# Two batches by four heads: regrouping the units of an fp32 RWKV-5 recurrence ahead of a hierarchical mixture of experts, with its start-up, gate loads and last expert reordered

## The chip, the cores and the metric

The kernel runs on one core of one Trainium2 chip. The metric is device time in microseconds (us) for one launch. The profile comes from one separate execution of the same program. All arithmetic is fp32.

## What is computed

The first block is the RWKV-5 recurrence with B=4 batches, H=8 heads, S=768 tokens and D=48 channels per head. For each batch and head:

```python
for t in range(S):
    cur = outer(u * k[t], v[t])            # the token's own term
    y[t] = r[t] @ (state + cur)
    state = w[:, None] * state + outer(k[t], v[t])
```

The result, read as x of 3072 tokens by 384 channels (8 heads of 48), goes into a mixture of 16 experts, in 4 groups of 4. A token takes the group with the largest of `x @ w_group`, then in that group the expert with the largest of `x @ w_expert[g]`. Both softmax weights multiply the result of its one expert, `relu(x @ w1) @ w2`, with 1024 hidden channels. Tokens have to be sorted by expert, and the results scattered back into their places.

## The kernel before

The recurrence is cut into chunks of 128 tokens. 24 units, or steps `s = 0..23`, stand in a loop `for s in range(NT)`. A unit is one batch, eight heads, 128 tokens; two units make a group `g = s // 2`, and the groups alternate between batches 0, 1 and batches 2, 3. The order of instructions on every engine is the order of the program text, written out by hand. Work of several units is interleaved: step s ends the products of unit s while it prepares units s+1 to s+4.

A unit goes through these functions:

- `load` (L323) issues two DMAs for each of r, k and v, one for each batch, with rows of 48 floats (192 bytes).
- On GpSimd (POOL), `own` (L489, L490) forms r*k*u and `scaled` (L493) forms k times the table `T2` of inverse powers of w.
- On TensorE (PE), `turn` (L511) transposes k and r; ScalarE (ACT) copies kT out (L520) and VectorE (DVE) multiplies rT by the powers `pw` (L522).
- `scores` (L536) forms k'r for each head, written as four quadrant products: two head halves `e` (48 of 64 rows each) by two key halves `z`. The lower key half (z=0) has 128 query columns, the upper (z=1) only 64, since key 64 and later don't reach an earlier query.
- `diagonal` (ACT, L561) and `diagonal_here` (DVE, L553) put the own term on the diagonal of `am`; `mask` (DVE, L543) copies the scores into `am` where the key is earlier than the query.
- `state` (L574) multiplies rT with the carried state R and `values` (L583) adds am times v; `values_out` (ACT, L612) copies the sum to `yT`. `update` (L594) and `carry` (DVE, L604) renew R.
- `rows_out` (L630, ACT L634) turns yT into rows of x. `gate_parts` (L619) multiplies yT by the gates' weights `gwp` in four matmuls and copies the result `lT` (L624). In a later step `gate_sum` (L644) sums its quarters into logits. `route_1` to `route_5` then choose the expert, and POOL scatters the rows into `x_sorted` with an indirect DMA (L230).

The constant `CLOSE` is 5: up to that step one unit less lies in preparation. PE has PSUM areas named PA, YB, MS, TR, RW, SB and LG; turns of k use TR and turns of r RW. PE, DVE and ACT each have one order and no dynamic choice.

Four DMAs, issued by `fill` (L439) at s = 5, 6, 7 and 8, zero parts of `x_sorted`, 392 KB each. `gates_in` (L406, L409) loads the gates' weights with five DMAs whose rows are 16 bytes. A check whether w is in the range that the kernel can treat is `out_of_range` (L752, L753) at s=0, summed over partitions by a matmul, `all_out_of_range` (L756). `turn_nothing` (L422) issues transposes whose results are not used.

At the end of the recurrence the experts run, 16 in an order fixed at run time by the counts. Their products are L1104 (up) and L1116 (down), their results leave by indirect DMAs (L1128). The last expert has few rows: `rows_down` (L240) multiplies, ACT scales (L244), and one indirect DMA of POOL (L245) writes rows of 384 floats to `out`.

## Time and profile before

| | us |
|---|---|
| median of 3 runs | 400.97 |
| lowest, highest | 399.18, 401.94 |
| the profiled execution, its own time | 402.09 |
| span of the profiled execution | 400.3 |
| TensorE busy (share of the span) | 388.7 (97%) |
| POOL busy | 201.0 (50%) |
| ACT busy | 180.4 (45%) |
| DVE busy | 153.4 (38%) |
| first and last `values` of the recurrence start at | 12.14, 127.36 |
| first expert product starts at | 129.48 |

PE is the matmul engine and PEld its loading of weights, which the profile lists apart. SP is the engine that issues most DMAs, and SPq the time that its queue took for them. A line of the timeline gives start and duration, engine, line of the code, operation, `out<-in`, tile shapes and, in brackets, how long the engine stood idle ahead of it and what ended that. Durations are those of one execution.

### The profile page before, as it was taken

How to read it: one execution, taken by the hardware profiler on the slowest of the kernel's cores; microseconds unless marked ns; L12 is line 12 of the kernel's file. 1: busy time of each engine (PE TensorE's matmuls, PEld its weight loads, DVE VectorE, ACT ScalarE, POOL GpSimd, SP SyncE). 2: the span in 40 equal slices, each digit the busy share in tenths (PEclk: the TensorE clock that was granted, in tenths of full speed). 3: DMA queues.
4: the chain of work that ended last, by engine and by line, in shares of the span. 5: the costliest groups of instructions: out<-in, count | busy, mean ns of one | idle time of the engine just before them, and what ended most of it. 6: DMA issues, size and time to landing. Idle time of an engine off the chain costs nothing.

```text
span 400.3 us, 10467 instructions
## 1 busy us (share of the span) xinstructions
PE 388.7 (97%) x3963; PEld 361.9 (90%) x3963; DVE 153.4 (38%) x405; ACT 180.4 (45%) x429; POOL 201.0 (50%) x265
## 2 busy tenths in 40 slices
PE   8999999999999999999999999999999999999992
PEld 6787899999888977899999999999999999999981
DVE  7887988888867602101202112111121221211110
ACT  4665888888875211432433424424244244244210
POOL 7999956999842412105162351532624524523542
PEclk9999999999999999999999999999999999999999
DMA  8998999995965977999999999999989999981000
GB/s 159 160 174 159 197 208 221 212 195 147 264 200 123 308 193 212 233 275 258 232 258 243 228 250 266 224 253 284 200 240 259 255 247 268 233 236 28 27 18 27
DMA packets 123118, 81.80 MB, mean 204 GB/s; under 512 B 96863, under 2 KB 114289, under 8 KB 123061
## 3 DMA queue, kind: packets, MB, share of 16 engines
q1 hardware_dynamic: 116019, 71.12, 77.1%
q0 software_dynamic: 4752, 9.55, 8.1%
q8 instruction: 32, 0.52, 0.6%
q10 hardware_dynamic: 2290, 0.40, 0.5%
q14 instruction: 25, 0.20, 0.2%
HBM read 69.89 MB, written 11.67 MB: 204 GB/s over the span
## 4 chain that ended last, share of the span: by engine, by line
issue 46%; PE 29%; POOL 18%; SPq 3%; DVE 2%; DMA 1%; POOLq 1%; ACT 0%
POOL out_dram L1128 16%; PE YB L583 6%; PE PA L536 6%; SPq L323 3%; PE TR L511 3%; PE YB L574 2%; PE YB L630 2%; PE RW L511 2%; PE MS L594 2%; PE TR L619 2%; PE MS L644 1%; DMA vt<-in_v_dram 1%; POOL out_dram L245 1%; PE TR L793 1%; DVE am L543 1%
## 5 line engine op out<-in xcount | busy, mean ns | idle before, releaser
L1128 POOL DMA_INDIRECT out_dram<-yt,idn x93 | 90.4, 972 | 137.1 <-DVE yt L1126 107.0
L1076 DVE STREAM_TRANSPOSE xe<-xg 128x672 f32<-128x672 f32 (+2 forms) x16 | 12.7, 796 | 121.0 <-DMA xg<-x_sorted 88.7
L1116 PE MATMUL YB<-hT,w2p 128*128 128x208 f32 (+10 forms) x336 | 58.7, 328 | 0.0
L1116 PE MATMUL PA<-hT,w2p 128*128 128x208 f32 (+10 forms) x336 | 58.1, 326 | 0.0
L1116 PEld LDWEIGHTS YB<-hT,w2p 128*128 128x128 f32 x336 | 55.8, 190 | 0.0
L1116 PEld LDWEIGHTS PA<-hT,w2p 128*128 128x128 f32 x336 | 55.3, 190 | 0.0
L561 ACT ACTIVATE am<-ident,du 128x128 f32<-128x128 f32 x152 | 50.5, 398 | 0.0
L1125 DVE STREAM_TRANSPOSE yt<-yT 128x672 f32<-128x672 f32 (+1 forms) x14 | 11.8, 842 | 80.4 <-ACT yT L1119 80.4
L1094 ACT COPY w2p<-w 128x1024 f32<-128x1024 f32 x42 | 41.1, 1045 | 3.0 <-DMA w<-in_moe_w_dram 3.0
L543 DVE COPY_PREDICATED am<-later,PA 128x1024 f32<-128x1024 int32 x24 | 31.7, 1323 | 10.8 <-PE PA L536 6.1
L1104 PE MATMUL MS<-xe,w 128*128 128x208 f32 (+12 forms) x192 | 32.8, 320 | 0.0
L1104 PE MATMUL TR<-xe,w 128*128 128x208 f32 (+12 forms) x192 | 32.8, 320 | 0.0
L1104 PE MATMUL RW<-xe,w 128*128 128x208 f32 (+12 forms) x192 | 32.8, 320 | 0.0
L1104 PE MATMUL SB<-xe,w 128*128 128x208 f32 (+12 forms) x192 | 32.7, 320 | 0.0
L1104 PEld LDWEIGHTS SB<-xe,w 128*128 128x128 f32 x192 | 30.8, 190 | 0.6 <-issue 0.2
L1104 PEld LDWEIGHTS MS<-xe,w 128*128 128x128 f32 x192 | 30.7, 190 | 0.0
L1104 PEld LDWEIGHTS RW<-xe,w 128*128 128x128 f32 x192 | 30.7, 190 | 0.0
L1104 PEld LDWEIGHTS TR<-xe,w 128*128 128x128 f32 x192 | 30.7, 190 | 0.0
L230 POOL DMA_INDIRECT x_sorted<-xt,place_i x16 | 16.1, 1003 | 23.6 <-DVE end L719 11.8
L536 PE MATMUL PA<-rT,kT 48*64 48x128 f32 (+1 forms) x736 | 25.6, 255 | 0.5 <-issue 0.5
L583 PE MATMUL YB<-am,vt 128*48 128x128 f32 x384 | 25.9, 277 | 0.1
L490 POOL TENSOR_TENSOR dg<-dg,ub 128x384 f32<-128x384 f32 x24 | 24.1, 1003 | 1.9
(220 smaller groups left out, 560.1 us busy)
## 6 DMA issues: line engine op xcount, KB each, us to landing
w<-in_moe_w_dram SPq DMA_DIRECT2D x128, 384.0 KB, 9.5
vt<-in_v_dram SPq DMA_DIRECT2D x24, 192.0 KB, 4.5
rp<-in_r_dram SPq DMA_DIRECT2D x23, 192.0 KB, 4.3
kt<-in_k_dram SPq DMA_DIRECT2D x22, 192.0 KB, 5.2
xg<-x_sorted SPq DMA_DIRECT2D x36, 85.8 KB, 10.3
x_sorted<-zeros SPq DMA_DIRECT2D x4, 392.0 KB, 4.7
out_dram<-yt,idn POOLq DMA_INDIRECT x93, 7.5
xg<-x_sorted SPq DMA_DIRECT2D x20, 73.5 KB, 8.9
```

The costliest lines, as they stand in the source:

```text
L230: ins = nc.gpsimd.indirect_dma_start(out=xs_dram, out_offset=bass.IndirectOffsetOnAxis(ap=place_i[:, i : i + 1], axis=0), in_=xt[:, i].rea ...
L490: nc.gpsimd.tensor_mul(dg, dg, ub)
L511: nc.tensor.transpose(ps[:, hc, :], two, ident)
L536: nc.tensor.matmul(PA[64 * z : 64 * (z + 1), e, P * hc + 64 * z : P * (hc + 1)], lhsT=kT[rows, hc, 64 * z : 64 * (z + 1)], rhs=rT[rows, hc ...
L543: nc.vector.copy_predicated(am[n % NAM], later.unsqueeze(1).unsqueeze(1).to_broadcast([P, 2, HC, P]).bitcast(I32), PA.rearrange("p e (h t) ...
L561: nc.scalar.mul(am[n % NAM][:, e, hc, :], ident, dus[n][:, i : i + 1])
L583: nc.tensor.matmul(y_at(e, hc), lhsT=vt[:, n % 2, 2 * hc + e, :], rhs=amn[:, e, hc, :], start=(n < 4 and hc < 2), stop=True, skip_group_ch ...
L1076: nc.vector.transpose(xe[:, :, 0:nb, :], xg[:, 0:nb, 0:QW].rearrange("p i (ko a) -> p ko i a", a=32))
L1094: nc.scalar.copy(o4[:, kk], v4[:, kk])
L1104: nc.tensor.matmul(ph[:, i, 0:n], lhsT=w1[:, ko, P * (f + i) : P * (f + i + 1)], rhs=xe[:, ko].rearrange("p i b -> p (i b)")[:, 0:n], star ...
L1116: nc.tensor.matmul(po[:, 0:n], lhsT=w2p[:, d, fo, :], rhs=hT[:, fo, 0:n], start=(fo == 0), stop=(fo == FO - 1))
L1128: ins = nc.gpsimd.indirect_dma_start(out=out_q, out_offset=bass.IndirectOffsetOnAxis(ap=idn[:, i : i + 1].bitcast(U32), axis=0), in_=yt[:, ...
```

## The change

The change regroups the units. A unit is now two batches by four heads (`hf = n % 2` says which four), and a group still has two units. In the second batch the two 64-token halves of a chunk lie swapped on the partitions. So for two of a unit's four pairs of heads (`hc` 0, 1: first batch) the lower 64 partitions hold the earlier tokens, and for the other two (`hc` 2, 3) the later ones. What follows from that in the code:

- `load_heads` issues three DMAs for a tensor of a group: 128 rows of the first batch, and twice 64 rows of the second. For group 0, r and k are split by heads as well.
- `scores` computes, by `columns_of`, 64 or 128 columns in each quadrant, in the order of heads 0, 2, 1, 3; the mask `LT` has four tables, the powers `PW`, `IW` and `T2` two. ACT makes the swapped ones by copies.
- `gate_parts` treats two units at once, in odd steps, and `gate_sums` two chunk columns, in even steps. In steps 3 and 4 both stand behind `state`; at s=5 the sums follow `gate_parts`' place. At s=22 `part` is issued alone.
- `own`, `scaled`, `sum_own`, `head` and `rows_out` take the new indices; `own` takes a buffer for each unit rather than for each group (three of them as before). `tok4`, the token numbers, is made by four iotas instead of one.

Beside it:

- `gates_in` loads the gates' weights as long rows (768 bytes) with two DMAs, earlier in SP's order; `gates_turned` turns them with four PE transposes and two ACT copies.
- The `turn_nothing` calls between the turns are gone (the first 13 transposes stay, into PA); `rows_of_table` makes the second half of T2 after `scores(0)`.
- ACT's copies that fill pads and blank `am` buffers move, in part to s=1.
- At s=4 `values_out` follows the diagonals, and the turn of k for unit 7 goes to PA.
- The zero fill of s=8 is issued at s=7, with the third.
- `out_of_range` moves to s=8 and its sum joins the count at s=14 (`count_and_range`); `in_range` and `go_on` follow there and at s=17.
- For the last expert `half_down` computes 192 columns at a time, each half scaled and scattered by itself.

The diff, cut to its core:

```diff
...
+    def half_down(hT, w2, i, n, z, po, yt):
+        cols = slice(DM // 2 * z, DM // 2 * (z + 1))
+        for fo in range(FO):
+            nc.tensor.matmul(
+                po[0:n, 0 : DM // 2], lhsT=hT[:, fo, 0:n], rhs=w2[:, fo, cols], start=(fo == 0), stop=(fo == FO - 1),
+                skip_group_check=True,
+            )
+        nc.scalar.mul(yt[0:n], po[0:n, 0 : DM // 2], tagA[i][0:n, 1:2])
...
-        def load_half(t, src, g, a, queue):
-            c, b = g // 2, 2 * (g % 2) + a
-            queue.dma_start(out=t[:, a], in_=src[b, :, P * c : P * (c + 1), :].rearrange("h t d -> t h d"))
+        def load_heads(t, src, g, queue, heads=slice(0, H)):
+            for b in range(2):
+                for rows, t0 in ((slice(0, P), 0),) if b == 0 else ((slice(0, 64), 64), (slice(64, P), 0)):
+                    t1 = P * (g // 2) + t0
+                    queue.dma_start(
+                        out=t[rows, b, heads],
+                        in_=src[2 * (g % 2) + b, heads, t1 : t1 + rows.stop - rows.start, :].rearrange("h t d -> t h d"),
+                    )
 
         def load(src, g, name, bufs):
             t = place(g, name, bufs)
-            for a in range(2):
-                load_half(t, src, g, a, nc.sync)
+            load_heads(t, src, g, nc.sync)
...
+        gates = kp[3].rearrange("p a h x -> p (a h x)")[0 : H * G + H, 0 : D * Eg].rearrange("p (d x) -> p d x", x=Eg)
+
+        def gates_in():
+            nc.sync.dma_start(
+                out=gates[0 : H * G].rearrange("p d x -> p (d x)"),
+                in_=moe_w_expert.rearrange("g (h d) x -> (g h) (d x)", d=D),
+            )
+            nc.sync.dma_start(
+                out=gates[H * G :].rearrange("p d x -> p (d x)"), in_=moe_w_group.rearrange("(h d) x -> h (d x)", d=D)
...
-        def gates_in():
-            wg = moe_w_group.rearrange("(h d) g -> d h g", d=D)
-            nc.sync.dma_start(out=gwp[0:D, :, 0:G], in_=wg)
-            for g in range(G):
-                we = moe_w_expert[g].rearrange("(h d) x -> d h x", d=D)
-                nc.sync.dma_start(out=gwp[0:D, :, G + Eg * g : G + Eg * (g + 1)], in_=we)
+        def gates_turned():
+            n = H * G + H
+            ps = MS.rearrange("p (x c) -> p x c", c=P)
+            for x in range(Eg):
+                nc.tensor.transpose(ps[0:D, x, 0:n], gates[:, :, x], ident[0:n, 0:n])
+            nc.scalar.copy(
+                gwp[0:D, :, G : G + GE].rearrange("p h (g x) -> p x g h", x=Eg),
+                ps[0:D, :, 0 : H * G].rearrange("p x (g h) -> p x g h", h=H),
+            )
+            nc.scalar.copy(gwp[0:D, :, 0:G].rearrange("p h x -> p x h"), ps[0:D, :, H * G : n])
...
+        for z in range(2):
+            half = slice(64 * z, 64 * (z + 1))
+            other = slice(64 * (1 - z), 64 * (2 - z))
+            nc.scalar.copy(LT[half, 2, half], LT[half, 0, half])
+            nc.scalar.copy(LT[half, 2, other], ones[half, 0:64] if z else nothing[half].to_broadcast([64, 64]))
         nc.scalar.copy(ub.rearrange("p h d -> p (h d)"), u_ps_all)
-        for n in (1, 2, 3):
-            if n < NRP - 1:
-                pads(rp, n)
-            pads(kp, n)
-
+        for t in (PW, IW):
+            for z in range(2):
+                nc.scalar.copy(t[:, 1, :, 64 * z : 64 * (z + 1)], t[:, 0, :, 64 * (1 - z) : 64 * (2 - z)])
+        for i in (1, 3):
+            nc.scalar.copy(LT[:, i, :], LT[:, i - 1, :])
...
+        def columns_of(hc, z):
+            return (64 * z, P) if hc < 2 else (0, 64 * (z + 1))
 
         def scores(n):
             kT, rT = rkT.pop((n, "kT")), rkT[n, "rT"]
-            for hc in range(HC):
+            for hc in (0, 2, 1, 3):
                 for e in range(2):
                     rows = slice(DP * e, DP * e + D)
-                    if n == 0:
+                    for z in range(2):
+                        c0, c1 = columns_of(hc, z)
                         nc.tensor.matmul(
-                            PA[:, e, P * hc : P * (hc + 1)], lhsT=kT[rows, hc, :], rhs=rT[rows, hc, :],
+                            PA[64 * z : 64 * (z + 1), e, P * hc + c0 : P * hc + c1],
+                            lhsT=kT[rows, hc, 64 * z : 64 * (z + 1)], rhs=rT[rows, hc, c0:c1],
                             start=True, stop=True, skip_group_check=True,
                         )
...
 
         def mask(n):
             nc.vector.copy_predicated(
-                am[n % NAM], later.unsqueeze(1).unsqueeze(1).to_broadcast([P, 2, HC, P]).bitcast(I32),
-                PA.rearrange("p e (h t) -> p e h t", t=P),
+                am[n % NAM].rearrange("p e h t -> p e (h t)"),
+                spread(LT.rearrange("p h t -> p (h t)"), 1, 2).bitcast(I32), PA,
...
+        def head(n, e, hc):
+            return hc // 2, 4 * (n % 2) + 2 * (hc % 2) + e
...
-        def gate_parts(n):
-            yT = yTs[n]
-            lT_ps = lT_at[n % 2 if n < 7 else 1]
-            for q in range(NQ):
-                e, j = q // 2, q % 2
-                nc.tensor.matmul(
-                    lT_ps[32 * q : 32 * (q + 1), :], lhsT=gwp[:, 4 * j + e, :], rhs=yT[:, e, j, :],
-                    start=True, stop=True, skip_group_check=True,
-                )
-            lT = mid[n] = pool.tile([P, P], FP32, tag="lT", bufs=3, name="lT")
-            nc.scalar.copy(lT, lT_ps)
+        def part(n):
+            for b in range(2):
+                for e in range(2):
+                    q = 2 * (n % 2) + e
+                    nc.tensor.matmul(
+                        TR[32 * q : 32 * (q + 1), b, :], lhsT=gwp[:, 4 * (n % 2) + e, :], rhs=yTs[n][:, e, b, :],
+                        start=True, stop=True, skip_group_check=True,
+                    )
+
+        def gate_parts(n, first=True):
+            if first:
+                part(n - 1)
+            part(n)
+            mid[n] = pool.tile([P, 2, P], FP32, tag="lT", name="lT")
+            nc.scalar.copy(mid[n], TR[:, 0:2, :])
...
-        def gate_sum(n):
-            nc.tensor.matmul(LG[:, n % 4, :], lhsT=mid.pop(n), rhs=sel, start=True, stop=True, skip_group_check=True)
+        def gate_sums(n):
+            lT = mid.pop(n)
+            for b in range(2):
+                nc.tensor.matmul(
+                    LG[:, n % 4 - 1 + b, :], lhsT=lT[:, b, :], rhs=sel, start=True, stop=True, skip_group_check=True
+                )
...
+        def rows_of_table(b, ps):
+            for hc in range(HC):
+                nc.tensor.transpose(ps[:, hc, :], IW[:, b, hc], ident)
+            nc.scalar.copy(
+                T2[:, b].rearrange("p (y e) d -> p y e d", e=2),
+                ps.rearrange("p y (e x) -> p y e x", x=DP)[:, :, :, 0:D],
+            )
+
+        whole_MS = MS.rearrange("p (h t) -> p h t", t=P)
+        turn(0, "rT", whole_MS)
         turn_first()
-        for hc in range(HC):
-            nc.tensor.transpose(rows_ps[:, hc // 2, P * (hc % 2) : P * (hc % 2 + 1)], iw[:, hc], ident)
-        nc.scalar.copy(
-            T2.rearrange("p (b y) d -> p b y d", b=2),
-            rows_ps.rearrange("p b (y x) -> p b y x", x=DP)[:, :, :, 0:D],
-        )
+        rows_of_table(0, RW)
         own(0, 0)
-        scaled(0, 1)
         own(0, 1)
-        scaled(0, 0)
         sum_own(0)
         diagonal_here(0)
         diagonal(0, 1, HERE - HC)
         scores(0)
-        nc.vector.tensor_mul(WL, pw[:, :, P // 2], pw[:, :, P // 2])
+        rows_of_table(1, whole_MS)
+        scaled(0, 1)
+        scaled(0, 0)
+        pads(rp, 1)
+        pads(kp, 1)
+
+        def blank(t):
+            nc.scalar.copy(diagonals(t)[:, 0:HERE], spread(nothing.to_broadcast([P, P]), 1, HERE))
+
+        blank(am[2])
+        mask(0)
+        half = spread(pw[:, :, P // 2].rearrange("p (f y) -> p f y", f=2), 2, 2)
+        nc.vector.tensor_mul(WL.rearrange("p f (b y) -> p f b y", b=2), half, half)
         nc.scalar.copy(wl, WL)
-        for t in am[2:4]:
-            nc.scalar.copy(diagonals(t)[:, 0:HERE], spread(nothing.to_broadcast([P, P]), 1, HERE))
-        mask(0)
-        turn_nothing(2)
         turn(1, "rT")
-        turn_nothing(4, TR)
         turn(1, "kT")
+        gates_turned()
...
+            if s == 1:
+                blank(am[3])
+                pads(rp, 2)
+                pads(kp, 2)
+                pads(kp, 3)
...
-            if s in (5, 6, 7, 8):
-                fill(s - 5)
+            for i in {5: (0,), 6: (1,), 7: (2, 3)}.get(s, ()):
+                fill(i)
...
-            values_out(s)
+            if s != CLOSE - 1:
+                values_out(s)
             if s == 0:
                 own_term(1)
-                out_of_range()
             for n, e, hc in waiting:
                 diagonal(n, e, hc, hc + 1)
             waiting.clear()
+            if s == CLOSE - 1:
+                values_out(s)
...
-            if s == 0:
-                all_out_of_range()
-                in_range()
...
-            for n in {4: (0, 1), 5: (2, 3), 6: (4,), 7: (5, 6)}.get(s, (s - 1,) if s > 7 else ()):
-                gate_sum(n)
+            summed = {4: 1, 5: 3, 7: 5}.get(s, s - 1 if s > 7 and s % 2 == 0 else None)
+            parts = {3: 1, 4: 3, 6: 5}.get(s, s if s > 6 and s % 2 == 1 else None)
+            if s > CLOSE and summed is not None:
+                gate_sums(summed)
             for c in range(NB - 1):
                 if s == first(c) + 2:
                     route_p(c)
                     if c == 2:
-                        count(12)
-            for n in {3: (0, 1), 4: (2, 3), 5: (4,), 6: (5, 6)}.get(s, (s,) if s > 6 else ()):
-                gate_parts(n)
+                        count_and_range(12)
+            if s >= CLOSE and parts is not None:
+                gate_parts(parts, s < NT - 1)
+            if s == NT - 2:
+                part(s)
+            if s == CLOSE:
+                gate_sums(summed)
...
+            if s < CLOSE:
+                if summed is not None:
+                    gate_sums(summed)
+                if parts is not None:
+                    gate_parts(parts)
             if s == CLOSE - 1:
-                turn(s + 3, "kT")
+                turn(s + 3, "kT", PA[:, 0].rearrange("p (h t) -> p h t", t=P))
                 turn(s + 3, "rT")
...
+                if p == last:
+                    for z in range(2):
+                        yt = pool.tile([P, DM // 2], FP32, tag="yh", name="yh")
+                        half_down(hTs[p], held(p)[1], 2 + i, SLOTS[i], z, next_of(downs), yt)
```

## The prediction

> **What bounds the kernel now.** I read the page's first row, then the chain of waits, then the windows cut at the starts of `values`, so that every row is one step, then the timeline inside some steps.
>
> ```profile
> span 400.3 us, 10467 instructions
> PE 388.7 (97%) x3963; PEld 361.9 (90%) x3963; DVE 153.4 (38%) x405; ACT 180.4 (45%) x429; POOL 201.0 (50%) x265
> ...
> issue 46%; PE 29%; POOL 18%; SPq 3%; DVE 2%; DMA 1%; POOLq 1%; ACT 0%
> ```
>
> TensorE is busy 97% and the chain is issue and PE for three quarters. Only fewer matmul passes, or the 3% in which PE stands still, can shorten this. The steps (us, busy PE, PEld, DVE, ACT, POOL, then clock, DMA share, GB/s):
>
> ```profile
> 12.14:16.86 4.72, 4.01 (x75) 3.28 (x75) 4.34 (x8) 2.69 (x7) 4.64 (x6) 1.00 1.05 199
> 16.86:20.95 4.09, 4.06 (x78) 3.44 (x77) 3.08 (x6) 2.33 (x6) 4.01 (x5) 1.00 0.55 63
> 30.50:37.84 7.34, 6.81 (x125) 5.57 (x121) 4.58 (x7) 3.41 (x10) 7.02 (x12) 1.00 0.92 172
> 37.84:44.46 6.62, 6.43 (x137) 5.37 (x136) 5.84 (x12) 5.75 (x19) 6.32 (x9) 1.00 0.89 193
> 59.73:64.51 4.78, 4.78 (x104) 4.31 (x102) 4.34 (x15) 4.16 (x14) 1.40 (x2) 1.00 0.96 208
> 74.63:79.42 4.79, 4.79 (x105) 4.32 (x106) 4.16 (x11) 4.06 (x14) 4.53 (x6) 1.00 0.90 201
> 129.48:393.00 263.52, 263.48 (x1616) 253.75 (x1612) 48.90 (x142) 87.50 (x161) 100.83 (x105) 1.00 0.88 218
> ```
>
> Rows 1 and 2 are steps 0 and 1, then come s=4, 5, 9, 12, and the experts. A step after s=8 is 4.78 us of PE without a gap; the experts are 263.5 us without a gap and the change leaves their matmuls as they are. DVE, ACT and POOL lie 0.25 to 0.7 us under PE in steady steps, so a saving beyond that meets the next engine. One steady step in PE's weight loads:
>
> ```profile
> 57.58 0.30 PEld L644 LDWEIGHTS MS<-sel,lT 128*128 128x128 f32 x2
> 57.91 0.16 PEld L619 LDWEIGHTS TR<-yT,gwp 128*32 128x32 f32 x8
> 58.27 0.86 PEld L536 LDWEIGHTS PA<-rT,kT 48*64 48x64 f32 x32 [0.20 <-issue]
> 58.99 0.56 PEld L574 LDWEIGHTS YB<-rT,R 48*48 48x48 f32 x16
> 59.73 0.82 PEld L583 LDWEIGHTS YB<-am,vt 128*48 128x48 f32 x16 [0.18 <-issue]
> ```
>
> From the starts: gate sum and parts 0.69 us together, scores 0.72, state 0.74.
>
> **What the Trainium skill says.** "TensorEngine Tiling (Array Packing)", Key Properties: tiles run independently, and changing the tiling mode drains the array. The trace agrees: sixteen scores matmuls over four quadrants take 0.72 us, and there is a gap of about 0.2 us ahead of scores and of values. So scores plus state last as long as their fullest quadrant. "TensorE: Matmul & The Clock Gate", Architectural detail: ScalarE and VectorE are strict FIFO; every moved ACT copy holds what stands behind it. "DMA: Bandwidth & Descriptors", Rules for kernel authors: two transfers to disjoint partition halves use the same engines and serialise; so a load cut by rows should cost no bandwidth, if each piece still reaches all of them. Its Specifications want 512 B or more for line rate; the loads have 192-byte rows before and after.
>
> **The change part by part.** Against the profiled execution, 402.09 us (span 400.3).
>
> *Scores.* Each fp32 matmul is two passes; in the trace 128 columns take 0.109 us a pass and 64 columns 0.058. Before, a lower quadrant (keys 0 to 63) has 4x2 passes of 128 columns in scores, and 2x2 in state: 12 x 0.109 = 1.31, and with the gap the measured 1.46. The upper has 8 x 0.058 + 4 x 0.109 = 0.90. With the second batch's halves swapped, both have 4 of each in scores: 4 x 0.109 + 4 x 0.058 + 4 x 0.109 = 1.10. Gain 0.2 us a step where PE bounds.
>
> *Gate matmuls.* An odd step has 8 part matmuls for two units (taken as 0.58) and no sum, an even step two sums (0.36) and no part, against 0.23 + 0.36 = 0.59 in every step. Even steps gain 0.24, odd ones nothing.
>
> *s=8 to 21.* 7 x (0.2 + 0.24) + 7 x 0.2 = 4.5. Steps 22 and 23 issue no scores; there unit 22's and 23's parts are issued singly and two sums stand for one: a loss of 0.2 each, 0.4.
>
> *s=3 to 6.* PE stands still here:
>
> ```profile
> 34.81 0.52 PEld L644 LDWEIGHTS MS<-sel,lT 128*128 128x128 f32 x4 [0.48 <-POOL zeros L880]
> ...
> 36.81 0.31 PEld L511 LDWEIGHTS TR<-ident,kp 128*128 128x128 f32 x3 [0.48 <-POOL dg L490]
> ```
>
> The sums and parts now come after state, and turn(7) goes to PA, so that it need not wait for the parts to leave TR. I take s=3 at 0.4 (its one stall is 0.48), s=4 at 1.2 (0.96 of stalls and 0.2 of scores), s=5 at 0.6 (0.2 of scores, and a unit's parts of 0.36; its wait for DVE stays), s=6 at 0.5 (the same, less an added wait), s=7 at nothing, since it now holds both parts and sums: together 2.7.
>
> *Steps 1 and 2* gain nothing: the chain there is values, yT, three diagonals, mask, values on ACT and DVE:
>
> ```profile
> 18.01 0.59 ACT L612 COPY yT<-YB 128x512 f32<-128x512 f32 x1 [1.88 <-PE YB L583]
> 18.49 0.98 ACT L561 ACTIVATE am<-ident,du 128x128 f32<-128x128 f32 x3
> 19.51 1.33 DVE L543 COPY_PREDICATED am<-later,PA 128x1024 f32<-128x1024 int32 x1 [0.97 <-ACT am L561]
> ```
>
> The copies and blanks moved to s=1 (1.87 us of ACT) just fill the 1.88 us of idle ahead of yT; with no cover they would cost up to 0.5.
>
> *Start-up.* One matmul goes from s=0:
>
> ```profile
> 16.54 0.30 PEld L756 LDWEIGHTS MS<-same,ones 128*128 128x128 f32 x2 [0.83 <-DVE R L604]
> 16.86 0.39 PEld L583 LDWEIGHTS YB<-am,vt 128*48 128x48 f32 x8
> ```
>
> Mask(1) ended at 16.25, so this cost values(1) about 0.5. But half of each batch's heads are in unit 1 now, and its T2 table comes from a second set of transposes after scores(0): ACT copy about 10.7 to 11.2, POOL's scaled(0,1) to 12.2, then turn(1), the gates' turns, and values(0) at about 12.97 instead of 12.14. From there the chain runs as before, 4.13 us without the removed matmul, to values(1) at 17.1 against 16.86: cost 0.25. New work on ACT (swapped copies of pw and iw, four of 0.3 to 0.4 us, and of the mask) may delay kT: I keep -0.3 to +1.0.
>
> *DMAs.* The gates' five transfers of 16-byte rows become two of long rows and leave SP's queue:
>
> ```profile
> 17.52 2.03 SPq L409 DMA_DIRECT2D gwp<-in_moe_w_expert_dram  x4
> ```
>
> with 0.71 for L406: 2.7 us of SP less, two issues of about 0.5 more. Each r, k, v tensor of a group takes three DMAs instead of two (128 rows and two of 64) with the same rows. The stream leads: kp of unit 12 is scaled at 52.4 and turned at 61.1, 8.7 us ahead. I put both at nothing.
>
> *Fill, POOL.* The last zero fill goes to s=7, ahead of where POOL stood:
>
> ```profile
> 63.07 1.20 POOL L230 DMA_INDIRECT x_sorted<-xt,place_i  x1 [7.65 <-DVE ohg L178]
> ```
>
> That wait ended a microsecond after the fill landed at 62.0. PE doesn't wait for it, so gain nothing, but it lets POOL follow. Four iotas for one: 0.7 us of POOL at s=2, covered by a margin of 1.1 at turn(8).
>
> *Range check, counts* (s=8, 14, 17): small, on DVE with room, nothing.
>
> *Tail.* The last expert's down goes in two column halves, each scaled and scattered:
>
> ```profile
> 393.18 0.58 ACT L244 ACTIVATE yd<-YB,tagA 96x384 f32<-96x384 f32 x1 [4.83 <-PE YB L240]
> 394.03 0.94 POOL L245 DMA_INDIRECT out_dram<-yd,idA  x1 [1.76 <-ACTq L1170]
> ```
>
> ACT's second half is 0.3 shorter and the transfer half as large, but POOL issues two scatters of 0.94. The first can start about 392.3, so the second issues on time: gain 0.3 (0 to 0.5).
>
> *Sum:* +0.25 (start) - 2.7 (s=3 to 6) - 4.5 (s=8 to 21) + 0.4 (s=22, 23) - 0.3 (tail) = -6.9. New semaphore waits (a second tile, a third DMA in each load: about 0.1 us each where the engine is full) I put at 0.5 in all. That leaves -6.3: 402.1 - 6.3 = 395.8. The profiled run lies 1.1 above the median of 400.97, so against that the forecast is **394.7**.
>
> **Rivals.**
>
> *The next engine sets the step* (0.20). For: the windows show ACT 4.06 to 4.16, DVE 4.16 to 4.34, POOL 4.53 busy in steps of 4.78, and in some steps their chain is near 4.64; an even step at 4.34 is under that. Against: ACT drops half the lT copies (0.26 each), and the buffers let steps borrow from one another over two steps. Then the fourteen steps give about 1.5 rather than 4.5: 397.7.
>
> *More is gained* (0.12). The new stalls don't come, start-up loses nothing, parts of 8 matmuls pack to 0.45 us (7 x 0.13 = 0.9), and 1.25 of the idle time of steps 18 to 20 (0.75 to 0.89 each, put down to issue) goes with the new order: 0.5 + 0.25 + 0.9 + 1.25 = 2.9 more, 391.8.
>
> *Slower: the load stream* (0.06). If a 64-row piece does not reach all DMA engines, or takes as long as a 128-row one, each tensor costs 3 half transfers for 2. SP issues loads without a break from 1 to 86 us, at about 155 GB/s. The recurrence loses its lead of 8.7 us once the stream is 8.7 / 52.4 = 17% slower, and is then paced by it. At 35% slower unit 12's kp comes at 52.4 x 1.35 = 70.7, 9.6 after the turn now starts; the steps after that still gain some 4: 401 + 9.6 - 4 - 0.3 = 406. Against: the rows have the same length and number, and the page on DMA has cuts by partition cost nothing.
>
> *It cancels* (0.04): ACT's filled idle time in s=1, start-up at +1.0, a POOL that is late at turn(8), and a pass that isn't shorter since the two quadrants share a column: 401. That the halves balance is settled by the code, so a change that doesn't do what it says has no more chance than this.
>
> **How the numbers follow.** Likeliest (0.58): 394.7, own range 393 to 396.5. The range 391.5 to 398.5 takes in that, most of the rivals of 397.7 and 391.8, and leaves out the slow and the cancelled one. This measurement can tell about 1%, 4 us: faster holds the likeliest case, the larger gain and a third of the partial one (0.58 + 0.12 + 0.07 = 0.77); within 1% the rest of the partial one and the cancelled one (0.17); slower 0.06.
>
> **What would show it.** Right: starts of scores and of values(s+1) 1.26 us apart instead of 1.46; even steps from s=8 at 4.35 us and odd ones at 4.6; first expert matmul at about 123; no stall at s=3 and 4; experts still 263.5. Wrong: "issue" or ACT, DVE, POOL waits ahead of PE in even steps (second bound); PE waiting for v or for a turn behind POOL's scaled at s=9 to 16, with loads landing later (the stream); values(0) after 13.5 (start-up).

## The result: half a percent slower

| | runs | median us | lowest to highest |
|---|---|---|---|
| before | 22 | 401.15 | 399.17 to 404.06 |
| changed | 22 | 402.81 | 400.05 to 405.62 |

The ratio is 1.0051, with a 95% interval of 1.0032 to 1.0070. Medians here and below are of all executions of a kernel, while the ratios compare only its undisturbed ones (those within 1.5% of its fastest), so that on the noisier chips of the experiments a ratio is not the quotient of two medians.

The profiled execution of the changed kernel has a span of 403.6 us (400.3 before). It was the longest of the 22 (405.62 us; 402.09 before), so the two traces lie 3.5 us apart where the medians lie 1.7 us apart. What a second trace of the same kernel (f1 below) doesn't show again is of this execution only. The page's first part, for the changed kernel:

```profile
span 403.6 us, 10589 instructions
PE 387.1 (96%) x3993; PEld 363.4 (90%) x3993; DVE 153.8 (38%) x408; ACT 182.9 (45%) x431; POOL 203.1 (50%) x269
```

PE is busy 1.6 us less and the span is 3.3 us more, so 4.9 us of new standing still came in. The windows of the same steps as before the change, cut at the starts of `values` (us, busy PE, PEld, DVE, ACT, POOL, then clock, DMA share, GB/s):

```profile
13.21:18.50 5.29, 3.62 (x74) 2.86 (x72) 2.61 (x4) 3.98 (x12) 1.38 (x3) 1.00 0.93 161
18.50:23.29 4.79, 3.87 (x77) 3.31 (x77) 3.54 (x5) 2.76 (x8) 4.63 (x6) 1.00 1.11 180
32.47:39.12 6.65, 6.61 (x125) 5.48 (x121) 5.08 (x8) 3.51 (x10) 5.32 (x12) 1.00 0.94 154
39.12:48.17 9.05, 7.08 (x129) 6.47 (x128) 6.29 (x14) 5.63 (x18) 8.75 (x12) 0.81 1.12 192
77.15:81.61 4.46, 4.46 (x101) 4.19 (x97) 3.95 (x11) 3.94 (x13) 4.13 (x6) 1.00 0.99 200
81.61:86.29 4.68, 4.68 (x112) 4.07 (x108) 4.37 (x14) 4.22 (x14) 4.42 (x5) 1.00 0.89 198
111.89:118.11 6.22, 6.22 (x109) 5.55 (x108) 3.12 (x6) 3.15 (x9) 4.94 (x14) 0.73 1.05 335
132.10:398.51 266.41, 264.18 (x1632) 256.43 (x1630) 49.02 (x144) 87.95 (x161) 102.91 (x107) 1.00 0.86 217
```

These are s=0, 1, 4, 5, an even step (12), an odd one (13), s=19 and the experts. The steady steps are shorter, 4.46 and 4.68 instead of 4.78. But steps 0 and 1 are longer, step 5 takes 9.05 instead of 6.62 and has a clock of 0.81, step 19 has one of 0.73, and the experts take 266.4 us to their last matmul instead of 263.7. PE's waits in that execution, by what it waited for (total, times, longest):

```profile
PE TR L569 <- POOL kp L542: 3.6, 3, 2.0
PE SB L1202 <- DVE xe L1174: 2.2, 1, 2.2
...
PE PA L592 <- issue: 1.3, 1, 1.3
PE RW L569 <- DMA rp<-in_r_dram: 1.3, 1, 1.3
PE YB L642 <- ACT kT L578: 1.2, 2, 0.9
```

The kernel before has no wait above 0.64 us but the one at the very start (1.4 us), which both have. Where the span of 3.3 us more comes from, by the starts of `values` in the two traces:

| stretch | before | changed | difference | predicted |
|---|---|---|---|---|
| to values(3) | 24.98 | 27.47 | +2.5 | +0.25 |
| s=3, 4 | 12.86 | 11.65 | -1.2 | -1.6 |
| s=5 | 6.62 | 9.05 | +2.4 | -0.6 |
| s=6, 7 | 10.49 | 10.21 | -0.3 | -0.5 |
| s=8 to 17 | 49.78 | 46.86 | -2.9 | -3.2 |
| s=18 to the first expert | 24.75 | 26.86 | +2.1 | -0.9 |
| experts to the last matmul | 263.66 | 266.41 | +2.75 | 0 |
| from there to the end | 7.16 | 5.07 | -2.1 | -0.3 |

The forecast's 0.5 us for new waits stands in no row. The gains of the steady steps are there. The losses lie at the start, at s=5, and around and behind the end of the recurrence.

**The start.** SP's DMAs in the changed kernel (start, time that the queue took, number):

```profile
1.39 4.00 SPq L348 DMA_DIRECT2D rp<-in_r_dram  x6
5.43 1.91 SPq L348 DMA_DIRECT2D rp<-in_k_dram  x3
7.39 1.93 SPq L348 DMA_DIRECT2D vt<-in_v_dram  x3
...
10.43 1.73 SPq L348 DMA_DIRECT2D kt<-in_k_dram  x3
```

The same load of group 1's k in the kernel before:

```profile
5.08 2.53 SPq L323 DMA_DIRECT2D kt<-in_k_dram  x2
```

Group 0's r and k are loaded by heads and by row halves, twelve DMAs, nine of them on SP. Each takes some 0.65 us of the queue (4.00 / 6 and 1.91 / 3), whether it carries 98 KB or 49 KB. So group 1's k is issued at 10.4 us; before it was at 5.1. Of these 5.3 us, 1.1 are the two gate loads, which now stand ahead of it. POOL, which before had no gap from 13 to 31 us, waits for k and r, and its own list then runs late until s=5. In the kernel before, the k of s=5's turn was ready at 37.59 us, 2.8 us ahead of its use, the shortest such lead among the units looked at (the next is 3.8):

```profile
36.59 1.00 POOL L493 TENSOR_TENSOR kp<-kt,T 128x384 f32<-128x384 f32 x1
40.37 0.66 PE L511 MATMUL TR<-ident,kp 128*128 128x128 f32 x4
```

In the changed kernel it is ready at 43.44. There PE waits for it, and its clock falls:

```profile
41.50:43.49 1.99, 0.02 (x2) 0.00 (x0) 1.06 (x3) 1.09 (x4) 1.99 (x3) 1.00 1.17 177
43.49:45.50 2.01, 2.01 (x10) 2.01 (x11) 1.46 (x4) 0.83 (x3) 1.87 (x4) 0.52 1.31 173
45.50:46.50 1.00, 1.00 (x7) 1.00 (x5) 0.66 (x1) 0.53 (x3) 1.00 (x2) 0.50 1.11 233
```

The wait of 2 us is followed by half speed until about 46.9 us, that is for 3.4 us. By an estimate (half of it) this costs 1.7 us more.

### The profile page after: what moved, and what is told of

The parts are those of the page before. It is cut to its first block, busy times and chain, and to the rows that moved or that the text cites. A ratio compares the mean times of both kernels' runs of the same rounds, so it can differ in the third digit from the quotient of the medians.

```text
span 403.6 us, 10589 instructions
## 1 busy us (share of the span) xinstructions
PE 387.1 (96%) x3993; PEld 363.4 (90%) x3993; DVE 153.8 (38%) x408; ACT 182.9 (45%) x431; POOL 203.1 (50%) x269
## 4 chain that ended last, share of the span: by engine, by line
issue 47%; PE 24%; POOL 20%; SPq 3%; DMA 2%; DVE 1%; ACT 1%; POOLq 1%; ACTq 0%
POOL out_dram L1226 16%; PE YB L642 5%; PE PA L592 4%; SPq L348 3%; PE TR L569 3%; DMA rp<-in_r_dram 2%; PE YB L630 2%; PE YB L693 2%; PE RW L569 2%; PE TR L677 2%; PE MS L653 1%; PE MS L710 1%; POOL dg L538 1%; POOL dg L539 1%; POOL out_dram L247 1%
## 5 line engine op out<-in xcount | busy, mean ns | idle before, releaser
L599 DVE COPY_PREDICATED am<-LT,PA 128x1024 f32<-128x1024 int32 x24 | 32.3, 1348 | 9.2 <-PE PA L592 6.2
L642 PE MATMUL YB<-am,vt 128*48 128x128 f32 x384 | 26.9, 283 | 1.2 <-ACT kT L578 1.2
L538 POOL TENSOR_TENSOR dg<-rp,kt 128x384 f32<-128x384 f32 x22 | 22.2, 1009 | 7.2 <-DMA rp<-in_r_dram 6.7
L642 PEld LDWEIGHTS YB<-am,vt 128*48 128x48 f32 x384 | 20.5, 126 | 5.6 <-issue 4.1
```

Of the source, the lines that this page charges most:

```text
L538: nc.gpsimd.tensor_mul(dg, four(raw[g, "r"], hf), four(raw[g, "k"], hf))
L599: nc.vector.copy_predicated(am[n % NAM].rearrange("p e h t -> p e (h t)"), spread(LT.rearrange("p h t -> p (h t)"), 1, 2).bitcast(I32), PA,)
L642: nc.tensor.matmul(y_at(e, hc), lhsT=vt[:, *head(n, e, hc), :], rhs=amn[:, e, hc, :], start=(n < 4 and hc < 2), stop=True, skip_group_chec ...
```

## The experiments

The experiments ran on several chips. On the chip of f1 to f4 the kernel before took 401.34 us, as in the measurement above; on those of all the other runs it took 418 to 430 us, so times are compared only on one chip. Transfers are slower there: e6, which is the kernel before up to its last expert, has `values(18)` at 104.7 us as in the first trace, but issues group 11's k at 86.2 us instead of 80.1 and starts its first expert at 137.0 instead of 129.5.

**f1, f2, f3, f4: one chip, kernel before 401.34 (11 runs), 6 runs each.**

f1 is the changed kernel, unaltered.

> The changed kernel unaltered, for its trace beside those of the next three on one chip. Theory A (SP's queue at the start): again a wait of some 2 us of PE for POOL's kp at s=5, PE's clock halved for some microseconds after it, and weights some 5 us later than in the kernel before; 1 to 3 us slower than before. If the waits of the first trace were chance, they are missing here and it is as fast as before or faster.

Measured: 404.94 us, ratio 1.0112 (1.0075 to 1.0150). Its trace repeats the first: values(3) at 27.48, a wait at s=5 of 1.85 us, then the halved clock:

```profile
46.50:48.56 2.06, 2.06 (x48) 1.71 (x44) 1.60 (x6) 1.39 (x5) 1.98 (x3) 0.50 1.04 221
```

So start and s=5 are no chance. Neither the 2.2 us ahead of an expert nor the issue wait and the low clock at s=18 and 19 recurred here.

f2 loads group 0 whole:

```diff
-        load_heads(raw[0, "r"], r, 0, nc.sync, slice(0, 4))
-        load_heads(raw[0, "k"], k, 0, nc.scalar, slice(0, 4))
-        load_heads(raw[0, "r"], r, 0, nc.sync, slice(4, 8))
-        load_heads(raw[0, "k"], k, 0, nc.sync, slice(4, 8))
+        load_heads(raw[0, "r"], r, 0, nc.sync)
+        load_heads(raw[0, "k"], k, 0, nc.scalar)
```

> The changed kernel with group 0's r and k loaded whole, in three DMAs each, r on SP and k on ACT (the edit of e1, once more, beside the changed kernel on the same chip). Theory A: no wait at s=5, values(6) about 3 us earlier than in the changed kernel, 3 to 5 us faster than it and 1 to 3 us faster than the kernel before. Theory B (the third DMA of every load): within 1 us of the changed kernel.

Measured: 402.12 us, 2.8 below f1 (six executions each, 400.4 to 404.2 and 403.7 to 408.7); against before 1.0021 (0.9996 to 1.0046). Step 5, in windows of f2:

```profile
41.06:47.17 6.11, 5.68 (x129) 4.92 (x128) 5.81 (x12) 5.24 (x17) 5.89 (x8) 1.00 0.97 197
```

6.11 us with a full clock, as against 9.16 in f1; the k of that turn was ready at 41.0 us instead of 43.6. So theory A holds for s=5: the split of twelve DMAs was the cause. For the start it does not hold. Group 1's k was issued at 8.3 us, and the first turn came later (2.4 us of wait for r, since all heads now arrive together). After that wait the clock was at half from 7.5 to 17.7 us, and values(3) started at 29.1; still values(6) came at 47.2 instead of 48.6. Nor does it hold for the whole: values(23) started at 126.9, 0.5 us ahead of the kernel before, but f2 is no faster than that. Its waits (first lines) show one behind the recurrence:

```profile
PE MS L567 <- DMA rp<-in_r_dram: 2.4, 1, 2.4
PE SB L1200 <- DVE xe L1172: 1.7, 1, 1.7
```

DVE's transpose `xe` waited for the fourth expert's rows, which stood behind weights in the queue:

```profile
197.72 0.88 DVE L1172 STREAM_TRANSPOSE xe<-xg 128x672 f32<-128x672 f32 x1 [11.90 <-DMA xg<-x_sorted]
```

f3 is f2 with the last expert in one piece (`rows_down` and one scatter).

> f2 with the last expert's product in one piece of 384 columns and one scatter, as before. Prediction's step: 0.3 us slower than f2. If the halves wait for ACT and POOL one after the other, 0 to 1 us faster than f2.

Measured: 402.81 us, 1.0029 (0.9993 to 1.0065): no difference from f2 that can be told. At s=5 it still had 1.4 us of the wait and took 6.91 us, with a full clock: whole loads shorten that wait and don't always remove it. Its trace has the recurrence at its shortest, values(23) at 124.4, 3 us ahead of the kernel before. Nothing of it reached the end: DVE stood still for the rows of the first experts, then PE for DVE:

```profile
130.69 0.58 DVE L854 STREAM_TRANSPOSE xeA<-xgA 128x384 f32<-128x384 f32 x1 [3.73 <-DMA xgA<-x_sorted]
```

and the first of the remaining experts started at 153.7 (152.2 before). SP issued these rows at 122.6 us, 4.3 us later than in the kernel before, although the recurrence ended 3 us earlier; the last weights ahead of them were issued 3.0 us later. Whether the third DMA of every load, which no run took out of the changed kernel, holds them back is not tested.

From the first remaining expert to the last matmul it was 241.0 us before, and 241.0 or 241.1 in f1, f3 and f4; it was 243.0 in f2 and 243.5 in the first trace of the changed kernel, where rows came late. From f1 to f3 the first expert starts 5.3 us earlier (132.29, 127.02) and the last matmul ends 1.9 us earlier (396.60, 394.68).

f4 undoes the balance of the quadrants in the changed kernel:

```diff
         def columns_of(hc, z):
-            return (64 * z, P) if hc < 2 else (0, 64 * (z + 1))
+            return (64 * z, P) if hc < 2 else (0, P)
```

> The changed kernel, but in the second batch's heads both key halves compute all 128 columns, so that the fuller quadrant has four products of 128 columns again, as before; the mask takes the same ones. The prediction's step (0.2 us a step, some 20 steps): scores and state take 1.46 us instead of 1.27, and the whole is 3 to 4 us slower than the changed kernel. If the next engine or the loads set the steps, no step gets longer and the time is the same within 1 us.

Measured: 404.94 us, the same as f1, although every step did get longer as the first theory had it. An even step in PE's weight loads, first the changed kernel (s=12), then f4:

```profile
80.34 0.75 PEld L592 LDWEIGHTS PA<-rT,kT 48*64 48x64 f32 x32
80.96 0.46 PEld L630 LDWEIGHTS YB<-rT,R 48*48 48x48 f32 x16
81.61 0.82 PEld L642 LDWEIGHTS YB<-am,vt 128*48 128x48 f32 x16 [0.18 <-issue]
```

```profile
80.27 0.86 PEld L592 LDWEIGHTS PA<-rT,kT 48*64 48x64 f32 x32
80.99 0.55 PEld L630 LDWEIGHTS YB<-rT,R 48*48 48x48 f32 x16
81.73 0.83 PEld L642 LDWEIGHTS YB<-am,vt 128*48 128x48 f32 x16 [0.18 <-issue]
```

1.27 and 1.46 us: the balance is worth 0.19 us a step. What f4 lost there it won back in the clock, in these traces: it has values(8) 2.5 us ahead of f1 and values(23) 0.2 us. Its wait at s=5 was 1.42 us and no halving followed:

```profile
43.70:46.94 3.24, 3.24 (x64) 3.02 (x65) 3.10 (x10) 2.53 (x8) 3.10 (x5) 1.00 1.01 194
```

Steps 5 and 6 took 12.2 us in f4 and 15.1 in f1. The mean granted clock over the six runs is 0.998 in f4 and 0.989 in f1; by an estimate, 0.0085 of 402 us is 3.4 us, as much as the balance saves in 18 steps. The expectation, 3 to 4 us slower than f1, was missed; six executions each (403.1 to 407.6, 403.7 to 408.7) don't exclude a difference of 2 or 3 us.

**e1, e3, e5, e6: kernel before 418.47 us on this chip.** e1 has f2's edit.

> The changed kernel, but group 0's r and k are loaded with all eight heads in three DMAs each, r on SP and k on ACT, instead of twelve DMAs of four heads of which nine are on SP. Theory A (SP's queue at the start: each DMA costs SP some 0.62 us whatever its size, so the split puts the whole load stream 4 to 5 us late): the first load of group 1's k is issued at about 6.5 us instead of 10.4, POOL's waits for r at 15 to 18 us and PE's wait of 2.0 us for POOL at s=5 go, values(3) starts at about 25.3 instead of 27.5, the wait of 2.2 us ahead of the fourth expert goes, and the time falls by 4 to 6 us below the changed kernel, to about 397 to 398. Theory B (the third DMA of every load slows the stream all along): at most 1 us is gained. Theory C (POOL's longer list and new waits): POOL stays late at s=5, at most 1 us is gained.

The wait at s=5 went here too (step 5 took 6.11 us, 8.87 in e3, which has the split loads), but the time was 420.13, ratio 1.0149 (1.0106 to 1.0192): here step 19 alone took 11.4 us, and the experts waited. The expectation in numbers was missed, at the start too: group 1's k was issued at 8.4 us and not at 6.5, and values(3) started at 27.5 and not at 25.3. With a full clock, steps 0 and 1 took 4.04 and 4.08 us, where the split loads have 5.29 and 4.79, but values(0) came at 15.2 instead of 13.2. So the split pays in the first two steps for what it gains ahead of them, and values(3) is late either way.

e3 is the changed kernel with the last expert in one piece.

> The changed kernel with the last expert's product in one piece of 384 columns and one scatter, as before. The prediction's step: 0.3 us slower than the changed kernel. The trace of the changed kernel: the end of the program came 5.1 us after the last matmul instead of 7.2, so 1 to 2 us slower. A theory in which the halves only moved the wait to GpSimd: no difference.

422.17 us, 1.0046 (0.9996 to 1.0097): against the kernel before; the changed kernel itself was not timed on this chip, so the halves are not judged by it.

e5 gives the kernel before the third DMA:

```diff
-            queue.dma_start(out=t[:, a], in_=src[b, :, P * c : P * (c + 1), :].rearrange("h t d -> t h d"))
+            for lo, n in ((0, P),) if a == 0 else ((0, 64), (64, 64)):
+                queue.dma_start(
+                    out=t[lo : lo + n, a], in_=src[b, :, P * c + lo : P * c + lo + n, :].rearrange("h t d -> t h d")
+                )
```

> The kernel before, but each load of r, k and v takes three DMAs (128 rows, and twice 64 rows of the second batch) as in the changed kernel, nothing else. Theory B (the third DMA costs): SP's stream of loads falls behind by 0.3 to 0.6 us a tensor, so by 8 us or more at group 11, weights come later and the time rises by 1 to 3 us. Theory A (only the start-up matters): three more DMAs before group 1's k, 1 to 2 us late there, then the same pace, and a time within 0.5 us of the kernel before.

419.59 us, 1.0046 (0.9987 to 1.0104): no difference that can be told. In the traces group 11's k is issued at 89.1 us, in e6, with two DMAs, at 86.2; the first weights at 98.6 and 95.4. So the third DMA costs the stream about 3 us over the whole recurrence, by one trace of each: less than theory B had, and not nothing.

e6 is the kernel before with `half_down` for the last expert.

> The kernel before with only the last expert's product in two column halves, each scaled and scattered by itself. The prediction's step: 0.3 us faster than before. The traces: the end comes 1 to 2 us earlier. A theory in which POOL's queue holds both scatters: no difference.

423.19 us, 1.0246 (1.0174 to 1.0318): slower, where all theories had the same or faster. In its trace ACT scaled the second half 1.8 us after the last matmul's modelled end, and the end came 8.3 us after that matmul (5.5 in e5). In the changed kernel, f1, f2 and f4 it came 4.9 to 5.2 us after it, in f3, with one piece, 5.4. In the other runs it came 6.2 to 7.1 us after it with halves (e1, g1 to g3, h1, h2, i1, i2), and with one piece 5.7 in e3 and 6.8 to 7.1 in g4, h3, i3 and the kernel before. So the halves' worth stays open, and the 2.1 us of the table's last row are not shown to be theirs.

**g1 to g4, h1 to h3, i1 to i3: is the rest lost behind the recurrence?** g1 (run again as h1 and i1) is f2 with each expert's rows fetched one expert earlier:

```diff
-            xg = xgs[p] = pool.tile([P, 8, QX], FP32, tag="xg", bufs=3, name="xg")
+            xg = xgs[p] = pool.tile([P, 8, QX], FP32, tag="xg", bufs=4, name="xg")
...
         fetch_rows(2)
+        fetch_rows(3)
         fetch_weights(2)
...
-            if 0 < p and p + 2 < GE:
-                fetch_rows(p + 2)
+            if 0 < p and p + 3 < GE:
+                fetch_rows(p + 3)
```

> f2 (group 0 loaded whole), and each expert's rows are fetched one expert earlier, into a fourth buffer, ahead of the second expert's weights. Theory D (behind the recurrence the transfers have almost no lead: the fourth expert's rows come 12 us after their issue, behind weights, so a recurrence that ends earlier only waits there): the wait of 1.7 us of PE ahead of the fourth expert goes, xe of that expert comes over 10 us ahead of its use, 1 to 2 us faster than f2 stood to the kernel before. If the weights themselves are what comes late, the wait moves to the weights (w2p or up) and nothing is gained.

> The kernel of g1 once more (group 0 loaded whole, experts' rows one expert earlier). Theory D (transfers behind the recurrence have no lead): no wait ahead of the fourth expert where f2 had 1.7 us, and 1 to 2 us less than f2 had against the kernel before, so up to 1 us faster than before. If the rows weren't it, the same as f2: 0.2% slower than before.

> The kernel of g1 and h1: group 0 loaded whole, experts' rows one expert earlier. Theory D: on a chip where the kernel before takes 401 us, no wait ahead of the fourth expert, and from 1 us faster to as fast as the kernel before, where f2 was 0.8 us slower. If the rows weren't it: as f2.

The wait ahead of the fourth expert is gone in all three traces. The time is not below the kernel before: 418.45 against 418.69 us, 1.0029 (0.9997 to 1.0061); as h1 430.89 against 429.58; as i1 431.84 against 427.55, 1.0325 (1.0154 to 1.0497; this ratio, and those of i2 and i3, rest on two executions of the kernel before). PE stood still ahead of later experts' `down` instead, 0.2 to 2.1 us at a time in i1. The profile puts that down to issue or to ACT's hT and yT; as ACT's copies of those experts' weights (w2p) waited 23.3 us in all for the DMA of w (3.0 before), it is read here as a wait for weights. On these chips the second half of the expectation came true; how it is on a chip as f2's was not measured.

g2 adds later gates (`gates_in` behind group 2's k, `gates_turned` at the end of s=1), and g3 does so with the split loads.

> g1, and the gates' weights loaded behind group 2's k and turned at the end of step 1 instead of ahead of values(0). Theory A: SP's stream is 1.6 us earlier for group 1's k and r, values(3) about 1 us earlier than in f2, and the time 0.5 to 1 us below g1. If POOL or ACT set the first steps, the same as g1.

> The changed kernel, with its split loads of group 0, and the late gates and early rows of g2. Theory A: values(0) as in the changed kernel (13.2 to 13.7), group 1's k issued at 9.4 instead of 10.4; the wait at s=5 shrinks by 1 us at most and stays; 1 to 2 us slower than g2. If the split was harmless and only gates and rows counted, as fast as g2.

g2: 420.01 us, 1.0076 (1.0032 to 1.0120); g3: 420.64, 1.0099 (1.0029 to 1.0169). Times don't tell them apart, and g2 is not below g1, as was expected, but 1.6 us above it. The traces do tell them apart: g3 with split loads waits 2.0 us at s=5 and takes 8.94 us there, g2 takes 6.11. That is a third pair for the split as the cause.

h2 (again as i2) is g2 with eight unused transposes ahead of the first turn.

> g2 (group 0 whole, gates late, rows early), and eight more transposes without use between the product for u and the first turn, so that PE is busy while group 0's r comes. If the halved clock of the first steps costs time, values(3) starts at 26 to 27 us and the time is 1 to 3 us below h1; if the first turn only waits for r, nothing changes, and if r lands early the eight transposes cost up to 1 us.

> The kernel of h2: as i1, with the gates' weights later and PE kept busy until group 0's r comes. In h2 values(3) started at 27.2 instead of 27.8 (h1) and no step had a halved clock, so 0.5 to 1 us faster than i1, and 1 to 2 us faster than the kernel before.

values(3) started at 27.2 us in both, 27.8 in h1 and i1. The times are not apart: 432.79 (h1 430.89), and as i2 430.76, 1.0253 (1.0082 to 1.0424).

g4 (again as h3 and i3) is the kernel before, and loads two pieces of weights twice. They are those of the second of the remaining experts (p = 1, counted from 0):

```diff
+        fetch_weights(1, range(2))
         fetch_rows(2)
         fetch_weights(2)
```

> The kernel before, but two pieces of the first expert's weights (2 x 384 KB) are loaded a second time, 3.6 us of the DMA stream at 218 GB/s. Theory D: in the trace of before the fourth expert's rows were ready 1.8 us ahead of their use (xe at 194.0 to 194.9, first product at 196.7), so PE waits 1 to 2 us there, and its clock may fall after it: 1 to 3 us slower than before. The prediction's view (experts bound by PE, transfers ahead): no difference.

> The kernel of g4 once more: the kernel before with two pieces of the first expert's weights loaded twice, 3.6 us of the stream. Theory D: PE waits 1 to 2 us ahead of the fourth expert, 1 to 3 us slower than before. The prediction's view (experts bound by PE): no difference.

> The kernel before with two pieces of the first expert's weights loaded twice (3.6 us of stream). Theory D: 1 to 3 us slower than before, with PE waiting ahead of an early expert (in g4 1.35 us ahead of the second). The prediction's view (experts bound by PE): no difference.

425.44 against 418.69 us, 1.0149 (1.0095 to 1.0203); 434.92 against 429.58; 434.11 against 427.55, 1.0406 (1.0269 to 1.0543). So 768 KB more in the queue made the kernel before 5.3 to 6.8 us slower at the medians, on chips with slow transfers. PE's wait came at that second expert, 3.3 to 4.0 us, and the twelve matmuls behind it took 4.58 us instead of 2.31; in h3 and i3 there were waits at later experts too. The edit puts the first pieces that this expert needs behind all its others, so that the wait is in part built in. It shows that a transfer that comes late there costs time, not how late it may come in the kernel before. No version was shown to beat the kernel before.

## Why the prediction was wrong

**"DMAs ... I put both at nothing" is the step that failed.** It counted bytes and bandwidth, and the lead of 8.7 us that the stream has at s=9. It didn't count SP's queue at the start, nor the lead at s=5, which is 2.8 us. That group 0's r and k "are split by heads as well" stood in the description and not in the sum. By the trace, group 1's k is issued 5.3 us later, behind nine DMAs of 0.65 us for group 0's r and k where two stood before, and the k of s=5's turn is ready 5.9 us later. At s=5 that became +2.4 us instead of -0.6. f1 and f2 show 2.8 us of it in the time. The Trainium skill's page "DMA: Bandwidth & Descriptors", Rules for kernel authors, says of two transfers to partition halves "Use one 128-partition transfer". The prediction took from it only that the bandwidth is the same; what the pieces cost here was the queue of the engine that issues.

**The start-up term was too small.** It had values(0) at 12.97 us and +0.25 at values(3); measured were 13.21 and +2.5. With whole loads it was no better: values(0) at 14.4 to 16.4, and +2.1 or more at values(3), in all nine such traces with the gates early or late. So the split is not what this loss comes from; that a unit now needs both batches of r and k before it can begin is a reading that no run isolates.

**A wait was priced at its length.** The half clock after it was not in any step. The Trainium skill's page "TensorE: Matmul & The Clock Gate", Part 1, What's actually happening, has a clock that falls after an idle window of some 3.4 us, and calls that window free-running. In this case shorter waits were followed by half the clock: 1.30, 1.85 and 1.97 us in the changed kernel, 2.3 to 2.5 us at the start of f2, f3 and g1. Others were not: 1.3 us at the start of e1 and h1, 1.42 (f3 and f4) and 2.19 us (at the fourth expert). The half clock lasted 3.4 us behind the waits of 1.30 and 1.97, 6.8 us in f1 and 10.2 us at the start of f2, close to one, two and three times the page's window. Of the 22 runs of the changed kernel the three with a mean clock of 1.000 took 400.05, 400.74 and 401.95 us, the five at 0.990 or less 403.5 to 405.6.

**"The experts are 263.5 us without a gap", carried over as fixed, is a floor and not the time.** In the trace of before the fourth expert's rows were transposed by 194.9 and used at 196.7: a lead of 1.8 us. A recurrence that ends 6 us earlier would have met the rows there unless they came earlier too. f2 (1.7 us) and f3 (3.7 us of DVE) show such waits, each in one trace. So the forecast gain of 6.3 us was more than this chain lets through; how much it lets through on that chip is not measured.

**The steady steps gained two thirds of what was forecast.** Scores and state were right: 1.27 us against 1.26 worked out, and f4 undoes exactly that. Parts of two units took 0.58 as taken. The two sums were taken as 0.36 and took 0.56 (79.78 to 80.34), although the old trace had 0.52 for two sums at 34.81; and sum and part together were taken as 0.59, where the prediction's own lines start 0.69 apart. An even step so gains 0.32 and not 0.44. An odd step gains 0.10 and not 0.20, for its parts now wait until ACT has copied kT out of TR; before, a sum stood between:

```profile
83.80 0.47 PEld L693 LDWEIGHTS YB<-ident,yT 128*128 128x128 f32 x4
84.44 0.39 PEld L677 LDWEIGHTS TR<-yT,gwp 128*32 128x32 f32 x16 [0.17 <-ACT kT L578]
```

That s=8 to 17 gave 2.9 of 3.2 is luck: 0.9 of it is s=17 (5.59 before, 4.69 now), where PE had stood still for 0.5 us; s=8 to 16 gave 2.0 of 3.0. The stalls of s=3 and 4 went, 1.2 us for 1.6.

**The rival that ended slower** was a stream paced at s=9 and later. It named SP's loads and the wrong place. The stream did fall behind: group 11's k is issued at 90.9 us instead of 80.1 (87.7 in f2), which is 13% slower where the rival needed 17%. PE lost to it at s=5, and not in the middle. The rival's chance of 0.06 was too small, as the stream had been seen to run without a break.

**Open.** The issue wait of 1.3 us and the clock of 0.73 at s=18 and 19 (before: 0.50 us at s=17 and 0.64 at s=18, no halving), seen in one trace of two; the loss at the start; what makes the rows of the first experts late in f3; and the worth of the halves at the tail. In f2's trace the 0.5 us of lead at values(23) is gone at the first remaining expert (152.2, as before), the experts take 2.1 us more, and the time from the last matmul to the end is 2.2 us shorter.

## What to carry to other kernels

Price a DMA twice, by its bytes and by its time in the queue that issues it, and look for the place where the stream's lead is shortest (here 2.8 us at s=5, not 8.7 at s=9): at the start a DMA more is a delay for all that follow. Before adding up PE's savings, look where transfers join behind the stage, and measure how early the data is there; that lead, not the savings, is what can be won. A new wait of over a microsecond on PE may cost as much again in clock, or nothing: here 1.97 us cost some 1.7 more and 1.42 us none.

## What was not expected of the hardware

- A DMA took SP's queue about 0.65 us at the start of the changed kernel, with 98 KB and with 49 KB alike. In the kernel before, with 192-byte rows too, DMAs of twice 98 KB took it 0.4 to 1.7 us each, so the time is not a constant.
- The clock fell to half after waits of 1.3 to 2.5 us, for 3.4, 6.8, 10 or more microseconds, in some executions and not in others.
- On a chip with slower transfers, engines stood still at s=19 with the profile naming no wait but issue: on i1 PE's `update` matmuls came in groups 0.7 us apart from 111 to 117 us. What held them is not shown.
